# One product (h w_in) in four column groups, spread by DMAs, in place of four products and sixteen transposing ones

## The chip, the core and the metric

The kernel runs on one core of a Trainium2 chip. The metric is the device time of one execution in microseconds (us), the median of several runs. The engines are TensorE (PE, matmuls; PEld is its weight load), VectorE (DVE), ScalarE (ACT), GpSimd (POOL) and SyncE (SP), which here issues the DMAs.

## The reference

Three stages follow each other over N = 12480 tokens of width 128:

```
h   = mab(I, x)                 # 32 inducing points attend to all tokens
x1  = mab(x, h)                 # each token attends to the 32 rows of h
        mab(q, kv): s = (q kv^T) / sqrt(128); a = softmax(s) (sum + 1e-9); a kv
y1  = prelu(x1 w_in, alpha) w_out          # w_in 128 x 2048, w_out 2048 x 128
out = relu(y1 w2_in)^2 w2_out              # the same shapes
```

All is fp32. The weights arrive as float64 and are converted on the chip.

## The kernel before

**First attention.** Seven groups of tokens are loaded, transposed on PE into xT and attended to. Beside them the pieces of w_in and w_out are converted from float64 to float32: `convs[k]` holds for each piece the parts MAG, LOW (both ACT), BITS, SIGN (DVE), ADD (POOL), and for w_out also REST (POOL, the product with 1 - alpha), HI (ACT, the fp32r high part) and LO (POOL, the low part). `convs[4]` to `convs[7]` are the four pieces of w_out. At its end hT stands in SBUF: h transposed, 128 x 32, four times beside each other.

**Second attention folded into the first MLP.** Softmax weights a of a token over 32 rows make x1 = a h, so x1 w_in = a (h w_in). The kernel therefore makes w1s, the high and low fp32r parts of h w_in stacked on the partitions (rows 0 to 63 high, twice; rows 64 to 127 low, twice), and a_s, the high and low parts of a, stacked likewise; one fp32r matmul of the two (line 618, `l1_a`) gives a chunk of 128 hidden units for a tile of tokens. w1s is made in four pieces of 512 columns: `make_w1s(k)` is an fp32 product on PE (line 531), `split_w1s(k, 0)` a cast on ACT, `split_w1s(k, 1)` a subtraction on DVE (line 536). Piece 0 is made ahead of the main loop, the others in it.

**The linear part of the PReLU.** alpha goes through v = (h w_in) diag(alpha) w_out, 32 x 128. It needs (h w_in) transposed: `step_wa` makes that in sixteen fp32 products (line 548), `scale_wa` copies it (ACT) and multiplies by alpha (POOL), `step_v` (line 592) makes v, `copy_v` and `split_v` give v_s, and `end_y1` adds a_s v_s.

**second_attention(tiles)** is a list of steps: scores (PE), transpose (DVE, line 465), maximum and subtraction (lines 470, 472), exp (ACT, 475), sums (lines 480 to 482, the product at 484), transpose back (488) and, for several tiles, `step_split`: casts and low parts, and four DMAs per tile to a_s. `first` is tile 0 alone, cut into three parts of 128 tokens; it has `step_spread` (PE, line 512) and `step_split_spread` (lines 519, 521) in place of DMAs. `second` is tiles 1 to 3. In `step_max` the subtraction is on DVE for `first` and in the main loop, and on POOL otherwise.

**The main loop** runs over steps s. The order in each engine's queue is the order of the program. Step s issues `l1_a(s)` (chunk s % 16 of tile s // 16), from step 24 on `l2_a(s - 24)` (the second MLP's first half), and the second halves `l1_b` (three fp32r matmuls, lines 628 to 630) five and later three steps behind, and `l2_b`. Each `l1_a` writes one of four PSUM banks in its first 24 steps (h1 and h2, two each); ACT's relu (line 622) and DVE's subtraction (line 624) empty it. A table `plan`, filled by `at(step, f)`, adds other work at the end of a step. `PIECES` says at which steps the pieces of w2_in and w2_out are converted (parts at s, s+1, s+2 and s+6). Their raw data lie in four buffers, so that the load of a piece waits for the ADD of the piece four before it. All these loads and the DMAs to a_s go through SP's one queue, in order.

Of the kernel before, what the change touches and what calls it, by code (L numbers as in the profile page):

```python
# [19 lines left out]
T = 512  # L20
# [5 lines left out]
Q = 4  # L26
# [4 lines left out]
def attention_then_two_mlps(ctx: ExitStack, tc, x, inducing, w_in, w_out, alpha, w2_in, w2_out, out):  # L31
# [327 lines left out]
    for g in range(last):  # L359
# [48 lines left out]
    sums(last)  # L408
    nnm = att.tile([P, 73], F32, name="nnm", tag="nnm")[:, :1]
    nc.vector.tensor_scalar_mul(nnm, nm[last], -1.0)  # L410
# [24 lines left out]
        den.unsqueeze(1).to_broadcast([P, Q, M]), op=ALU.mult,  # L435
    )
    convs[5][REST]()
    convs[4][LO]()
    convs[7][BITS]()

# [3 lines left out]
    def second_attention(tiles, cuts=None):  # L444
# [32 lines left out]
        def step_sum():  # L477
            a = v["a"]
            sm = att.tile([P, 3 * T // M], F32, name="sm", tag="sm")[:n, : w // M]
            nc.vector.reduce_sum(sm, a, axis=AX.X)  # L480
            nc.vector.tensor_scalar_add(sm, sm, 1e-9)
            nc.vector.reciprocal(sm, sm)
            mult = nc.vector.tensor_tensor if cuts else nc.gpsimd.tensor_tensor
            mult(a, a, sm.unsqueeze(2).to_broadcast([n, w // M, M]), op=ALU.mult)
# [5 lines left out]
        def new_a_s(t):  # L490
            a_s[t] = columns(att.tile([P, T], F32R, name="a_s", tag="a_s", bufs=5), wide[t])
            return a_s[t]

        def step_split():

            hi = att.tile([P, T], F32R, name="a_hi", tag="a_hi")
            nc.scalar.copy(hi[:n, :w], v["t"][:n, :w])
            lo = att.tile([P, T], F32R, name="a_lo", tag="a_lo")
            pool_lo(lo[:n, :w], v["t"][:n, :w], hi[:n, :w])
            for i, t in enumerate(tiles):  # L500
                d = new_a_s(t)
                for k in range(4):
                    nc.sync.dma_start(
                        out=f32(d[k * M : (k + 1) * M]),
                        in_=f32((lo if k % 2 else hi)[i * M : (i + 1) * M, :w]),
                    )
# [9 lines left out]
        def step_split_spread():  # L516

            d = a_s[tiles[0]] = new_a_s(tiles[0])[: 3 * M]
            nc.scalar.copy(d, v["b"][: 3 * M, :tw])
# [6 lines left out]

    w1_bank = {}

    def make_w1s(k):
        w1_bank[k] = x_banks[k]() if k < 2 else y2_bank()  # L530
        nc.tensor.matmul(w1_bank[k], hT, w_in_sb[:, k * 512 : (k + 1) * 512], start=True, stop=True)

    def split_w1s(k, low):
        dst, b = w1s[:, k * 512 : (k + 1) * 512], w1_bank[k]
        if low:
            nc.vector.tensor_tensor(dst[64:], b[64:], f32(dst[64:]), op=ALU.subtract)  # L536
        else:
            nc.scalar.copy(dst, b)

    wa = att.tile([P, NCH, M], F32, name="wa", tag="a_s", bufs=5)  # L540
    wa_bank = []

    def step_wa(chunks):
        if not wa_bank:
            wa_bank.append(y2_bank())
        for c in chunks:
            n = min(P, (c + 1) * M)
            nc.tensor.matmul(
                wa_bank[0][:, (c + 1) * M - n : (c + 1) * M], w_in_sb[:, c * P : (c + 1) * P], hT[:, :n],
                start=True, stop=True,  # L550
            )

    def scale_wa():
        nc.scalar.copy(wa, wa_bank[0].rearrange("p (c j) -> p c j", j=M))
        nc.gpsimd.tensor_tensor(wa, wa, al.unsqueeze(2).to_broadcast([P, NCH, M]), op=ALU.mult)

    first = second_attention([0], [0, P, 2 * P])
    second = second_attention([1, 2, 3])
    first[0]()
    make_w1s(0)  # L560
    step_wa(range(15, 3, -1))
    run(first[1:4])
    split_w1s(0, 0)
    convs[5][HI]()
    stage1.close()
    run(first[4:6])
    split_w1s(0, 1)
    convs[6][SIGN]()
    first[6]()
    second[0]()  # L570
    first[7]()
    convs[7][SIGN]()
    convs[6][ADD]()
    convs[5][LO]()
    convs[6][REST]()
    second[1]()
    second[2]()
    convs[7][ADD]()
    convs[7][REST]()
    load_w("w2_in", 0)  # L580
    load_w("w2_in", 1)
    load_w("w2_out", 0)
    load_w("w2_in", 2)

# [3 lines left out]
    def step_v():  # L588
        v_bank.append(y2_bank())
        for c in range(NCH):  # L590
            q = c % Q
            nc.tensor.matmul(
                v_bank[0][q * M : (q + 1) * M, :P], wa[:, c, :], w_out_sb[:, c, :],
                start=(c < Q), stop=(c >= NCH - Q), tile_position=(0, q * M),
            )
# [80 lines left out]
    def l2_b(i):  # L676
# [21 lines left out]
    PIECES = [  # L698
        (8, "w2_in", 0), (13, "w2_in", 1), (18, "w2_out", 0), (21, "w2_in", 2),
        (23, "w2_out", 1), (25, "w2_in", 3), (28, "w2_out", 2), (32, "w2_out", 3),  # L700
    ]
# [5 lines left out]

    at(0, step_wa, range(3, -1, -1))
    at(0, make_w1s, 1)
    at(1, split_w1s, 1, 0)  # L710
    at(1, split_w1s, 1, 1)
    at(1, second[3])
    at(2, scale_wa)
    at(2, make_w1s, 2)
    at(2, split_w1s, 2, 0)
    at(2, convs[6][HI])
    at(2, convs[6][LO])
    at(3, second[4])
    at(4, split_w1s, 2, 1)
    at(5, second[5])  # L720
    at(5, make_w1s, 3)
    at(5, split_w1s, 3, 0)
    at(6, convs[7][HI])
    at(6, convs[7][LO])
    at(7, split_w1s, 3, 1)
    at(7, second[6])
    at(10, step_v)
# [83 lines left out]
```

## Time and profile before

| | us |
|---|---|
| median of 3 runs (lowest to highest) | 968.28 (968.27 to 969.36) |
| the profiled execution | 969.27 |
| its span in the trace | 967.5 |
| PE busy in the span | 954.3 |
| DVE busy | 658.3 |
| ACT busy | 728.5 |
| POOL busy | 535.4 |

The span is the time from the first to the last instruction of the trace; the profiled execution's own time is a little longer. Busy times are sums over the span. Matmuls overlap, and their ends in the trace are modelled, so PE's busy time is no measure of its peak. Every fp32 matmul appears as two instructions.

### The profile page before, as it was taken

The page shows a single profiled execution, that of the slowest core. Times are in us where ns is not written, and L with a number is a line of the kernel's source. Part 1 is how long each engine was busy: PE and PEld are TensorE (multiplying, and loading weights), DVE is VectorE, ACT ScalarE, POOL GpSimd, SP SyncE. Part 2 cuts the span into 40 slices and gives each one's busy share as a digit, 9 for nine tenths or more (in the row PEclk, how much of TensorE's full clock was granted, in tenths as well). Part 3 has the DMA queues.
Part 4 walks back from the last instruction along what each step waited for, and adds up shares of the span by engine and source line. Part 5 has one row for each costly group of instructions (what it writes and reads, how often), then busy time and mean ns, then how long its engine had stood idle before and what let it go on. Part 6 is the DMA issues. An engine that isn't in the chain of part 4 may idle for free.

```text
span 967.5 us, 13705 instructions
## 1 busy us (share of the span) xinstructions
PE 954.3 (99%) x4577; PEld 791.6 (82%) x4577; DVE 658.3 (68%) x1027; ACT 728.5 (75%) x1335; POOL 535.4 (55%) x438
## 2 busy tenths in 40 slices
PE   9989999999999999999999999999999999999997
PEld 7767899887888887888887888887888887888886
DVE  6878876666766666676666776666766666766677
ACT  6678787777777777777777777777777777777775
POOL 2458765555565555565555565555566555566520
PEclk9999999999999999999999999999999999999999
DMA  8531002000001000002000002000002000001001
GB/s 327 163 111 45 9 7 48 11 3 8 12 14 41 12 1 12 12 9 47 11 1 12 12 3 53 12 1 12 12 1 55 11 1 12 12 1 23 11 2 23
DMA packets 65159, 28.28 MB, mean 29 GB/s; under 512 B 53584, under 2 KB 58304, under 8 KB 65088
## 3 DMA queue, kind: packets, MB, share of 16 engines
q1 hardware_dynamic: 64032, 27.27, 11.3%
q8 instruction: 36, 0.59, 0.3%
q14 instruction: 35, 0.29, 0.1%
q10 hardware_dynamic: 1056, 0.13, 0.1%
HBM read 14.80 MB, written 6.39 MB: 22 GB/s over the span
## 4 chain that ended last, share of the span: by engine, by line
PE 96%; ACT 1%; DVE 1%; POOL 1%; issue 0%; DVEq 0%; ACTq 0%
PE y L630 18%; PE y L629 18%; PE y L628 18%; PE h L628 9%; PE h L630 9%; PE h L629 9%; PE h L618 9%; PE h L273 1%; PE ms L287 1%; PE ms L457 1%; PE y L646 1%; PE y L337 1%; ACT g1h L622 0%; DVE g1l L624 0%; PE ms L95 0%
## 5 line engine op out<-in xcount | busy, mean ns | idle before, releaser
L673 POOL TENSOR_TENSOR g2l<-sq,g2h 128x512 fp32r<-128x512 f32 (+2 forms) x376 | 474.0, 1261 | 345.9 <-ACT g2h L671 327.4
L624 DVE SCALAR_TENSOR_TENSOR g1l<-h,g1h 128x512 fp32r<-128x512 f32 (+2 forms) x400 | 269.6, 676 | 238.2 <-ACT g1h L622 232.3
L622 ACT ACTIVATE g1h<-h 128x512 fp32r<-128x512 f32 (+2 forms) x400 | 234.6, 588 | 151.1 <-PE h L618 149.0
L664 DVE TENSOR_TENSOR sq<-h,r 128x512 f32<-128x512 f32 (+2 forms) x400 | 270.8, 677 | 46.1 <-ACT r L662 7.5
L662 ACT ACTIVATE r<-h 128x512 f32<-128x512 f32 (+2 forms) x400 | 234.8, 587 | 59.0 <-PE h L630 12.5
L671 ACT CAST g2h<-sq 128x512 fp32r<-128x512 f32 (+2 forms) x400 | 240.2, 600 | 3.7 <-DVE sq L664 3.7
L618 PE MATMUL h<-a_s,w1s 128*128 128x512 f32 (+2 forms) x400 | 156.2, 391 | 4.4 <-DVE w1s L536 2.0
L628 PE MATMUL h<-y1h,w2i_hi 128*128 128x512 f32 (+2 forms) x400 | 154.3, 386 | 1.5 <-DVE g1l L624 1.5
L630 PE MATMUL y<-g1l,wo_hi 128*128 128x512 f32 (+2 forms) x400 | 154.2, 385 | 0.0
L629 PE MATMUL y<-g2h,w2o_lo 128*128 128x512 f32 (+2 forms) x400 | 153.7, 384 | 0.2 <-POOL w2o_lo L215 0.2
L628 PE MATMUL y<-g1h,wo_hi 128*128 128x512 f32 (+2 forms) x400 | 153.8, 385 | 0.0
L629 PE MATMUL y<-g1h,wo_lo 128*128 128x512 f32 (+2 forms) x400 | 153.8, 385 | 0.0
L630 PE MATMUL h<-y1l,w2i_hi 128*128 128x512 f32 (+2 forms) x400 | 153.7, 384 | 0.0
L628 PE MATMUL y<-g2h,w2o_hi 128*128 128x512 f32 (+2 forms) x400 | 153.6, 384 | 0.0
L629 PE MATMUL h<-y1h,w2i_lo 128*128 128x512 f32 (+2 forms) x400 | 153.6, 384 | 0.0
L630 PE MATMUL y<-g2l,w2o_hi 128*128 128x512 f32 (+2 forms) x400 | 153.6, 384 | 0.0
L618 PEld LDWEIGHTS h<-a_s,w1s 128*128 128x128 f32 (+1 forms) x400 | 75.1, 188 | 27.0 <-DVE sq L664 5.0
L628 PEld LDWEIGHTS h<-y1h,w2i_hi 128*128 128x128 f32 x400 | 75.1, 188 | 16.8 <-DVE g1l L624 1.9
L629 PEld LDWEIGHTS y<-g2h,w2o_lo 128*128 128x128 f32 x400 | 75.1, 188 | 15.3 <-POOL w2o_lo L215 0.5
L628 PEld LDWEIGHTS y<-g2h,w2o_hi 128*128 128x128 f32 x400 | 75.2, 188 | 14.7
L629 PEld LDWEIGHTS h<-y1h,w2i_lo 128*128 128x128 f32 x400 | 75.1, 188 | 14.6
L630 PEld LDWEIGHTS y<-g2l,w2o_hi 128*128 128x128 f32 x400 | 75.1, 188 | 14.0 <-DVE g2l L673 0.2
(134 smaller groups left out, 688.5 us busy)
## 6 DMA issues: line engine op xcount, KB each, us to landing
out_dram<-o SPq DMA_DIRECT2D x82, 64.0 KB, 2.0
raw<-in_moe_w_in_dram SPq DMA_DIRECT2D x8, 512.0 KB, 5.2
xg<-in_x_dram SPq DMA_DIRECT2D x8, 512.0 KB, 9.2
raw<-in_moe_w_out_dram SPq DMA_DIRECT2D x8, 512.0 KB, 4.1
a_s<-a_hi SPq DMA_DIRECT2D x42, 64.0 KB, 2.0
a_s<-a_lo SPq DMA_DIRECT2D x42, 64.0 KB, 2.0
xg<-in_x_dram SPq DMA_DIRECT2D x4, 256.0 KB, 3.7
x_last<-in_x_dram SPq DMA_DIRECT2D x2, 512.0 KB, 10.6
```

What stands on the lines that cost most here:

```text
L273: nc.tensor.transpose(b[:, k * p : (k + 1) * p], x_t[g][:p, i, k, :], ident[:p, :p])
L287: nc.tensor.matmul(b[i * M : (i + 1) * M, :n], indT, xT[:, t0 : t0 + n], start=True, stop=True, tile_position=(0, i * M),)
L618: nc.tensor.matmul(b[:, :w], w1s[: a.shape[0], c * P : (c + 1) * P], a, start=True, stop=True)
L622: nc.scalar.activation(hi, b[:, :w], AF.Relu)
L624: nc.vector.scalar_tensor_tensor(lo, b[:, :w], 0.0, f32(hi), op0=ALU.max, op1=ALU.subtract)
L628: nc.tensor.matmul(b, w_hi, hi, start=start, stop=False)
L629: nc.tensor.matmul(b, w_lo, hi, start=False, stop=False)
L630: nc.tensor.matmul(b, w_hi, lo, start=False, stop=stop)
L662: nc.scalar.activation(r, b, AF.Relu)
L664: nc.vector.tensor_tensor(sq, b, r, op=ALU.mult)
L671: nc.scalar.copy(hi, sq)
L673: (nc.vector if i >= total - LAG2 else nc.gpsimd).tensor_tensor(lo, sq, f32(hi), op=ALU.subtract)
```

## The change

The product (h w_in) is made once more compactly. Piece 0 of w1s is made as before. All four pieces are also made by four fp32 matmuls with 32 columns of hT, each in a column group of PE of its own, so that piece k stands on partitions 32k to 32k + 31 of one bank. ACT copies this bank to `w1f` (fp32) and `w1h` (fp32r), POOL makes the low part `w1l`. Nine DMAs on SP's queue bring pieces 1 to 3 to w1s (high, high, low for each). The transposed form for alpha comes from four PE transposes of `w1f`, and `scale_wa` is one DVE product that reads PSUM. w1s and a_s have 96 rows in place of 128 (high, high, low against high, low, high), so `step_split` sends three DMAs per tile. Around it, SIGN, ADD, REST and HI of piece 6 and BITS of piece 7 move to other places, transpose, maximum and subtraction of tiles 1 to 3 move into steps 0 and 1 of the loop, five idle products (`keep_busy(5)`) are added, and the w2 pieces start up to two steps earlier.

```diff
     convs[5][SIGN]()
...
+    convs[6][SIGN]()
     convs[5][REST]()
     convs[4][LO]()
-    convs[7][BITS]()
+    convs[6][ADD]()
+    convs[6][REST]()
...
-                for k in range(4):
+                for k in range(3):
                     nc.sync.dma_start(
                         out=f32(d[k * M : (k + 1) * M]),
...
+    def make_first_w1s():
+        w1["first"] = h1_bank()
+        nc.tensor.matmul(w1["first"], hT, w_in_sb[:, :512], start=True, stop=True)
+
+    def make_w1():
+        b = w1["bank"] = h2_bank()
+        for k in range(Q):
+            nc.tensor.matmul(
+                b[k * M : (k + 1) * M], hT[:, :M], w_in_sb[:, k * 512 : (k + 1) * 512], start=True, stop=True,
+                tile_position=(0, k * M),
+            )
+
+    def first_w1s_low():
+        nc.vector.tensor_tensor(w1s[64:, :512], w1["first"][64:], f32(w1s[64:, :512]), op=ALU.subtract)
+
+    def copy_w1():
+        nc.scalar.copy(w1s[:, :512], w1["first"])
+        w1["f"] = att.tile([P, 512], F32, name="w1f", tag="a_s", bufs=5)
+        nc.scalar.copy(w1["f"], w1["bank"])
+        w1["hi"] = att.tile([P, 512], F32R, name="w1h", tag="a_s", bufs=5)
+        nc.scalar.copy(w1["hi"], w1["bank"])
+        w1["lo"] = att.tile([P, 512], F32R, name="w1l", tag="a_s", bufs=5)
+        pool_lo(w1["lo"], w1["f"], w1["hi"])
+
+    def spread_w1s():
+        for k in range(1, Q):
+            for r, v in enumerate(("hi", "hi", "lo")):
+                nc.sync.dma_start(
+                    out=f32(w1s[r * M : (r + 1) * M, k * 512 : (k + 1) * 512]), in_=f32(w1[v][k * M : (k + 1) * M, :])
+                )
+
+    def step_wa():
+        b = w1["wa"] = y2_bank()
+        for q in range(Q):
+            nc.tensor.transpose(b[:, q * P : (q + 1) * P], w1["f"][:, q * P : (q + 1) * P], ident)
+
     def scale_wa():
-        nc.scalar.copy(wa, wa_bank[0].rearrange("p (c j) -> p c j", j=M))
-        nc.gpsimd.tensor_tensor(wa, wa, al.unsqueeze(2).to_broadcast([P, NCH, M]), op=ALU.mult)
+        wa = w1["wa scaled"] = att.tile([P, Q, Q, M], F32, name="wa", tag="a_s", bufs=5)
+        nc.vector.tensor_tensor(
+            wa, w1["wa"].rearrange("p (q k j) -> p q k j", q=Q, k=Q),
+            al.rearrange("p (k q) -> p q k", q=Q).unsqueeze(3).to_broadcast([P, Q, Q, M]), op=ALU.mult,
+        )
...
     first[0]()
-    make_w1s(0)
-    step_wa(range(15, 3, -1))
+    make_first_w1s()
+    make_w1()
     run(first[1:4])
-    split_w1s(0, 0)
+    copy_w1()
+    keep_busy(5, idle_bank)
     convs[5][HI]()
+    run(first[4:6])
+    step_wa()
     stage1.close()
-    run(first[4:6])
-    split_w1s(0, 1)
-    convs[6][SIGN]()
+    first_w1s_low()
+    convs[7][BITS]()
     first[6]()
     second[0]()
     first[7]()
     convs[7][SIGN]()
-    convs[6][ADD]()
-    convs[5][LO]()
-    convs[6][REST]()
-    second[1]()
-    second[2]()
-    convs[7][ADD]()
-    convs[7][REST]()
+    convs[6][HI]()
     load_w("w2_in", 0)
     load_w("w2_in", 1)
     load_w("w2_out", 0)
+    spread_w1s()
+    convs[5][LO]()
+    convs[7][ADD]()
+    convs[7][REST]()
+    convs[6][LO]()
     load_w("w2_in", 2)
...
     PIECES = [
-        (8, "w2_in", 0), (13, "w2_in", 1), (18, "w2_out", 0), (21, "w2_in", 2),
-        (23, "w2_out", 1), (25, "w2_in", 3), (28, "w2_out", 2), (32, "w2_out", 3),
+        (7, "w2_in", 0), (11, "w2_in", 1), (16, "w2_out", 0), (20, "w2_in", 2),
+        (22, "w2_out", 1), (25, "w2_in", 3), (28, "w2_out", 2), (32, "w2_out", 3),
     ]
...
-    at(0, step_wa, range(3, -1, -1))
-    at(0, make_w1s, 1)
-    at(1, split_w1s, 1, 0)
-    at(1, split_w1s, 1, 1)
-    at(1, second[3])
+    at(0, second[1])
+    at(1, second[2])
+    at(2, second[3])
     at(2, scale_wa)
-    at(2, make_w1s, 2)
-    at(2, split_w1s, 2, 0)
-    at(2, convs[6][HI])
-    at(2, convs[6][LO])
     at(3, second[4])
-    at(4, split_w1s, 2, 1)
+    at(4, convs[7][HI])
+    at(4, convs[7][LO])
     at(5, second[5])
-    at(5, make_w1s, 3)
-    at(5, split_w1s, 3, 0)
-    at(6, convs[7][HI])
-    at(6, convs[7][LO])
-    at(7, split_w1s, 3, 1)
-    at(7, second[6])
+    at(6, second[6])
     at(10, step_v)
```

## Rows read from the trace of the kernel before

**Rows 1.** Busy time of each engine by stretch: us, (instructions), clock, DMA.
```profile
52.00:56.00 4.00, 2.11 (x10) 1.38 (x9) 3.35 (x7) 3.01 (x8) 3.62 (x5) 1.00 0.39 125
56.00:60.00 4.00, 4.00 (x36) 3.32 (x39) 3.72 (x8) 2.84 (x6) 1.99 (x2) 0.65 0.10 23
...
200.00:400.00 200.00, 200.00 (x891) 164.11 (x890) 131.98 (x194) 150.58 (x269) 113.69 (x89) 1.00 0.07 12
```

**Rows 2.** PE in order of time: start, us, engine, line, operation [idle before, releaser].
```profile
39.72 1.13 PE L531 MATMUL h<-w_in_sb,hT 128*128 128x512 f32 x2
...
40.69 2.84 PE L548 MATMUL y<-hT,w_in_sb 128*128 128x128 f32 x24
...
44.20 0.95 PE L457 MATMUL ms<-xT,hT 128*32 128x448 f32 x6
...
45.42 0.44 PE L618 MATMUL h<-a_s,w1s 96*128 96x384 f32 x1 [0.27 <-DVE a_s L521]
...
55.84 0.41 PE L618 MATMUL h<-a_s,w1s 96*128 96x384 f32 x1 [1.73 <-DVE w1s L536]
...
58.91 1.87 PE L592 MATMUL y<-w_out_sb,wa 128*32 128x128 f32 x32
...
64.55 0.36 PE L618 MATMUL h<-a_s,w1s 128*128 128x448 f32 x1
...
73.31 0.44 PE L628 MATMUL h<-y1h,w2i_hi 128*128 128x384 f32 x1 [1.50 <-DVE g1l L624]
```

**Rows 3.** DVE in order of time, 39 to 56 us.
```profile
39.24 0.98 DVE L203 TENSOR_SCALAR mag<-mag 128x512 int32<-128x512 int32 x1
...
40.79 0.69 DVE L472 TENSOR_TENSOR a<-a,mx 96x128 f32<-96x128 f32 x1
...
42.18 0.17 DVE L481 TENSOR_SCALAR sm<-sm 96x4 f32<-96x4 f32 x1
...
42.59 0.29 DVE L484 TENSOR_TENSOR a<-a,sm 96x128 f32<-96x128 f32 x1
...
43.97 0.69 DVE L207 SCALAR_TENSOR_TENSOR mag<-raw,mag 128x512 int32<-128x512 int32 x1
...
45.39 1.24 DVE L207 SCALAR_TENSOR_TENSOR mag<-raw,mag 128x512 int32<-128x512 int32 x1
...
46.66 0.65 DVE L465 STREAM_TRANSPOSE a<-ms 96x448 f32<-96x448 f32 x1
...
47.34 0.61 DVE L470 TENSOR_REDUCE mx<-a 96x14 f32<-96x448 f32 x1
...
47.88 1.03 DVE L624 SCALAR_TENSOR_TENSOR g1l<-h,g1h 128x384 fp32r<-128x384 f32 x2
...
53.65 0.66 DVE L481 TENSOR_SCALAR sm<-sm 96x14 f32<-96x14 f32 x1
...
55.00 0.69 DVE L536 TENSOR_TENSOR w1s<-y,w1s 64x512 fp32r<-64x512 f32 x1
```

**Rows 4.** ACT in order of time, the cast of the first piece of w1s.
```profile
41.74 0.56 ACT L538 CAST w1s<-h 128x512 fp32r<-128x512 f32 x1
```

**Rows 5.** POOL in order of time, 38 to 55 us.
```profile
38.89 1.04 POOL L225 TENSOR_TENSOR aw<-w_out_sb,al 128x512 f32<-128x512 f32 x1
...
39.89 1.45 POOL L215 TENSOR_TENSOR wo_lo<-aw,wo_hi 128x512 fp32r<-128x512 f32 x1
...
44.80 1.28 POOL L210 TENSOR_TENSOR w_out_sb<-mag,raw 128x512 int32<-128x512 int32 x1 [3.46 <-ACT a_s L519]
...
53.00 1.28 POOL L215 TENSOR_TENSOR wo_lo<-aw,wo_hi 128x512 fp32r<-128x512 f32 x1
```

**Rows 6.** SP queue in order of time: one DMA of 56 KB to a_s.
```profile
59.24 0.58 SPq L503 DMA_DIRECT2D a_s<-a_hi  x1
```

**Rows 7.** DMA issues: operation, count, KB each, median us to landing.
```profile
a_s<-a_hi SPq DMA_DIRECT2D x42, 64.0 KB, 2.0
...
al_raw<-in_moe_alpha_dram SPq DMA_DIRECT2D x1, 8.0 KB, 8.2
```

More of the change, by code (lines that the diff above doesn't have):

```diff
@@ L408, in attention_then_two_mlps @@
     sums(last)
-    nnm = att.tile([P, 73], F32, name="nnm", tag="nnm")[:, :1]
+    nnm = att.tile([P, 57], F32, name="nnm", tag="nnm")[:, :1]
     nc.vector.tensor_scalar_mul(nnm, nm[last], -1.0)
@@ L478, in step_sum @@
             a = v["a"]
-            sm = att.tile([P, 3 * T // M], F32, name="sm", tag="sm")[:n, : w // M]
+            sm = att.tile([P, 4 * T // M], F32, name="sm", tag="sm")[:n, : w // M]
             nc.vector.reduce_sum(sm, a, axis=AX.X)
@@ L490, in new_a_s @@
         def new_a_s(t):
-            a_s[t] = columns(att.tile([P, T], F32R, name="a_s", tag="a_s", bufs=5), wide[t])
+            a_s[t] = columns(att.tile([P, T], F32R, name="a_s", tag="a_s", bufs=5), wide[t])[: 3 * M]
             return a_s[t]
@@ L516, in step_split_spread @@
         def step_split_spread():
-            d = a_s[tiles[0]] = new_a_s(tiles[0])[: 3 * M]
+            d = new_a_s(tiles[0])
             nc.scalar.copy(d, v["b"][: 3 * M, :tw])
@@ L524, in second_attention @@
         return steps + ([step_spread, step_split_spread] if cuts else [step_split])
[L527 to L547, printed above, removed]
+    w1 = {}
+    def make_first_w1s():
[4 more added lines that the diff above has]
+        for k in range(Q):
             nc.tensor.matmul(
-                wa_bank[0][:, (c + 1) * M - n : (c + 1) * M], w_in_sb[:, c * P : (c + 1) * P], hT[:, :n],
-                start=True, stop=True,
-            )
@@ L592, in step_v @@
             nc.tensor.matmul(
-                v_bank[0][q * M : (q + 1) * M, :P], wa[:, c, :], w_out_sb[:, c, :],
+                v_bank[0][q * M : (q + 1) * M, :P], w1["wa scaled"][:, q, c // Q], w_out_sb[:, c, :],
                 start=(c < Q), stop=(c >= NCH - Q), tile_position=(0, q * M),
```

## The prediction

> **What bounds the kernel now.** I read the page first, which puts TensorE (PE) on nearly all of the chain that ended last, then the busy time by stretch. The reader is to see there that from about 104 us on PE is busy all the time at full clock (200.00 of 200 us in the row shown), so nothing that the other engines do there can shorten the run, and that PE is short of work at the start of the main loop: in 52 to 56 us it worked 2.11 of 4, and in 56 to 60 the granted clock was 0.65, which costs 4 x 0.35 = 1.4 us of its full speed [rows 1]. So the change is worth what it does to the start of the main loop. Then the timelines. The loop's first matmul (line 618) stands at 45.42, released by VectorE (DVE), not by PE; the first chunk of token tile 1 (step 16) comes at 64.55, and the first of the second MLP (step 24) at 73.31 [rows 2]. Whatever moves these points and is not given back before 104 us moves the end by as much.
>
> Steps 0 to 16 take 64.55 - 45.42 = 19.13 us. PE's own step is four matmuls: between the end of step_v (58.91 + 1.87 = 60.78) and 64.55 lie five steps and split_v, 0.75 us each [rows 2]. Sixteen would be 12.0 us. The rest is fp32 work of the old w1s and wa products, one wait of 1.73 us for the low half of a w1s piece, and waits for banks, which DVE empties at 1.03 / 2 = 0.5 us per chunk [rows 2, 3].
>
> **What goes.** On PE, inside the loop: three 512-column products (line 531, 1.1 us each with their end) and four of line 548; 24 instructions of it, 12 products, took 2.84, so 0.24 each, 0.95 for four [rows 2]. Together 3 x 1.1 + 0.95 = 4.2 us. On DVE, three lows of 0.69 = 2.1 us [rows 3]. On ScalarE (ACT), three casts of 0.56 and the copy of wa, 2.2 us [rows 4]. On POOL the product of wa with alpha. The wait of 1.73 goes with its cause.
>
> **What comes.** PE ahead of the loop: one 512-column product (1.1), four column groups (the scores of line 457, three groups of 448 columns in six instructions, took 0.95 in all [rows 2]; I take 1.1 for four of 512; one after another would be 4.4, and the six-instruction row excludes it), five idle products at 0.24 and four transposes (between nothing and 0.95, the price of the four products of line 548; I take 0.5). They end near 43.6 and have to be done before the spread of tile 0, which I put at 44.7 below: hidden. Before, twelve products and one of line 531 filled the same gap, so PE was not the limit there either. ACT makes three copies in place of one, 0.56 each, from 42.1 to 43.6, in a stretch in which it waits for the next a_s: hidden. In the loop DVE gets scale_wa (PSUM and SBUF input, bounded by 0.49 and 0.69 of rows of that kind; I take 0.69) and the subtraction of the tiles 1 to 3 (no longer on POOL; 96 x 448, own time near the 0.65 of the transpose of that shape), and the transpose and maximum of these tiles (0.65, 0.61) move into the loop's queue from a place just ahead of it [rows 3]. DVE's balance in the loop is 0.69 + 0.65 - 2.1 = -0.8 us.
>
> **The prologue's chain gets longer.** This is the step that I weigh most. DVE instructions that read only SBUF are long exactly when POOL is at work. The shift of line 203 at 39.24 took 0.98 and ended 0.29 after POOL's product of 38.89 (at 39.93); the subtraction at 40.79 took 0.69 for 96 x 128 and ended at 41.48, just after POOL's low half ended at 41.34, while the product of the same shape at 42.59, with POOL idle, took 0.29; the sign step takes 0.69 at 43.97, POOL idle, and 1.24 at 45.39, POOL busy; the small tensor_scalar of line 481 takes 0.17 at 42.18 and 0.66 at 53.65, ending at 54.31 where POOL ended at 54.28 [rows 3, 5]. In the kernel before, POOL is idle from 41.34 to 44.80 (3.46 us), which is where the chain of tile 0 runs [rows 5]. The change fills this gap: ADD and REST of piece 6 and the low half of w1 go to POOL there, and the 0.69 sign step stands on DVE in front of the chain. Walking it: the sign step gets through at 39.8 and ends at 40.5 (the shift ended at 40.22); POOL's low half ends at 41.6 in place of 41.34, the subtraction at 41.8, exp at 42.1; line 481 waits for ADD's end at 43.0 (before: 42.35), line 484 waits for REST's end at 44.05 and ends at 44.2 (before: 42.88). The loop's first matmul stood 2.54 after that end (45.42 - 42.88); I take off 0.1, since the products of line 548, which end at 43.53, no longer stand in front of the spread: 44.2 + 2.44 = 46.6. If nothing of this bites it comes at 45.2, the sign step being shorter than the held shift. These are the ends, +1.2 and -0.2; I take +1.2, because every such row beside a busy POOL is long.
>
> The Trainium skill, "SBUF — State Buffer", section "Who interferes with whom", says that a VectorE instruction with two SBUF inputs or in a two-port mode and a GpSimd instruction lock each other out for a whole instruction, and that one with a PSUM input does not contend. The rows above agree (0.29 against 0.69, 0.17 against 0.66); by the rule the chain is 1.2 us later, without it 0.2 earlier, and scale_wa, which reads PSUM, would be free of it.
>
> **The nine DMAs.** The queue of SP issues one such transfer per 0.6 us and it lands 2.0 us later [rows 6, 7]. Ahead of them stands the load of w2_out 0, which waits for ADD of piece 6 at 43.0, no longer for 46.1. The low half of w1 is done on POOL at 45.5; its first transfer goes then, with the two high ones out before. Group 1 lands at 47.5, group 2 at 49.3, group 3 at 51.1. Steps 4, 8 and 12 need them. The nearest worse row is the 8 KB transfer that took 8.2 us behind large loads [rows 7]: then group 1 lands near 53.8.
>
> **The loop.** DVE in order from 46.5: the sign step of piece 7, held by POOL to 47.1, ends at 47.7; bank 0 at 48.2; transpose 48.85; bank 1 at 49.35; maximum 49.9; subtraction, held to 50.05, 50.65; bank 2 at 51.15; scale_wa 51.85; bank 3 at 52.35; sums 53.35; bank 4 at 53.85. Banks are reused after four chunks, so PE does step 4 at 48.3 (group 1 is there, 0.8 us ahead) and step 8 at 53.9; before, step 8 stood at 55.84, after the wait. From there PE is the limit: eight steps of 0.75 and step_v, 1.87 at the lower clock of its row and half of it, 0.9, at the full one, which end at 60.8 to 61.8; I take 61.4. PE works less than half of 47 to 54 us, less than in 52 to 56 of before, which came just ahead of the lower clock; so I expect a stretch at 1.2 GHz here too and charge 0.8 for it, near the middle of nothing and 1.4 [rows 1]. Step 16 at 62.2: 2.3 us earlier than 64.55.
>
> **After step 16.** The conversions of w2 start one or two steps earlier. Their work is the same and PE's 8.76 us to step 24 contain waits of 1.50 and others; I credit 0.5, between nothing (conversions still crowd DVE) and 1.5 (the wait at 73.31 goes [rows 2]). Three rows of a_s per tile in place of four saves SP's time alone: PE is full there, and a matmul over 96 rows costs what one over 128 costs (0.44 at 45.42, 0.36 for a wider one at 64.55 [rows 2]). Later groups: nothing.
>
> **Sum.** -2.3 - 0.5 = -2.8 us. The profiled execution took 969.27, its span and 1.77 around it; so 966.5 there. The median of the runs is 0.99 below the profiled one: 968.28 - 2.8 = 965.5.
>
> **Rivals.** (1) POOL does not hold the chain: 1.4 us more gained, 964.1, and 963.3 if the clock stays up as well. For it: the five long rows overlap POOL only by my reading of their ends. Against: every overlapped SBUF-only row is long. 0.2. (2) The gain is given back to the clock: the first stretch costs its whole 1.4 (0.6 more than charged) and a second one as much; 965.5 + 2.0 = 967.5. For it: PE idles more in 47 to 54 us than before. Against: from step 8 on it has work without end. 0.2. (3) Slower: the spread lands late. Group 1 decides: it has 0.8 us to spare, and from there each microsecond delays step 4 and the fourteen behind it. At 53.8, twelve steps at 0.75 and step_v at 0.9 end at 63.7, with two low stretches at 66.5, up to 2 us later than before: 970. Against: the a_s transfers, of the same size, take 2.0 us in the median [rows 7]. 0.1. My forecast holds 0.5, with a range of its own of 964.2 to 966.8.
>
> **Chances.** 0.2% is 1.94 us, about what can be told from no change here; the border stands at 966.3. Rival 1 and most of the forecast (0.42) are faster: 0.62. Rival 2 and the rest of the forecast: 0.28 same. Rival 3: 0.10 slower. The range leaves out rival 3 and the lower part of rival 1: 963.0 to 968.5.
>
> **What would show it.** In the profile after: line 484 of tile 0 ends near 44.2 and not at 42.9; first line 618 near 46.6; no fp32 product of the w1s or wa kind after it; step 16 near 62; step 24 near 70.5; from 104 us nothing changed. The prediction is wrong if step 4 waits for w1s from a DMA, if the clock is low for over 4 us, or if the conversions make new waits between steps 16 and 40.

## The result and the profile after

The change made the kernel slower: 976.89 us in the median against 968.77, ratio 1.0083 (95% interval 1.0066 to 1.0101). The forecast was 965.5. The profiled execution took 976.8 us, its span is 975.0, 7.5 longer than before.

Busy time by stretch, of the changed kernel (columns as in [rows 1]):

```profile
52.00:56.00 4.00, 2.93 (x9) 2.83 (x10) 3.93 (x9) 2.60 (x6) 0.80 (x2) 0.50 0.46 131
56.00:60.00 4.00, 4.00 (x44) 3.76 (x43) 2.42 (x5) 3.09 (x7) 2.60 (x3) 0.70 0.08 20
...
200.00:400.00 200.00, 200.00 (x882) 162.73 (x881) 131.01 (x192) 149.26 (x266) 112.41 (x89) 1.00 0.06 11
```

The last row matters most. PE is busy all the time, at full clock, and waits for nobody, as before [rows 1]; but in the same 200 us it did 882 matmuls and not 891. The busy share cannot show that; the count can.

PE in order of time, of the changed kernel (line 636 is the loop's first matmul, 618 before; 646 to 648 are 628 to 630; 610 is step_v):

```profile
47.69 0.96 PE L636 MATMUL h<-a_s,w1s 96*128 96x384 f32 x4 [1.00 <-DVE a_s L523]
49.30 0.44 PE L636 MATMUL h<-a_s,w1s 96*128 96x384 f32 x1 [0.66 <-DVE g1l L642]
...
55.80 0.52 PE L636 MATMUL h<-a_s,w1s 96*128 96x384 f32 x1
...
59.19 1.08 PE L610 MATMUL y<-w_out_sb,wa 128*32 128x128 f32 x32
...
64.04 0.37 PE L636 MATMUL h<-a_s,w1s 96*128 96x448 f32 x1
...
72.76 0.45 PE L646 MATMUL h<-y1h,w2i_hi 128*128 128x384 f32 x1 [0.22 <-DVE g1l L642]
...
300.94 0.39 PE L648 MATMUL y<-g2l,w2o_hi 128*128 128x512 f32 x1
301.16 0.40 PE L636 MATMUL h<-a_s,w1s 96*128 96x512 f32 x1
301.40 0.40 PE L646 MATMUL h<-y1h,w2i_hi 128*128 128x512 f32 x1
301.63 0.40 PE L647 MATMUL h<-y1h,w2i_lo 128*128 128x512 f32 x1
301.87 0.39 PE L648 MATMUL h<-y1l,w2i_hi 128*128 128x512 f32 x1
302.10 0.39 PE L646 MATMUL y<-g1h,wo_hi 128*128 128x512 f32 x1
```

Step 16 comes at 64.04 and step 24's second MLP at 72.76, 0.5 us earlier than before each [rows 2]. The last six rows show where the time went: the matmul of 96 rows and the three behind it start 0.23 to 0.24 apart. Over 17 steps from 300 us on, the mean from one start to the next is 0.232, 0.237, 0.233 and 0.230 us behind these four, and 0.227 behind the other six; in the kernel before it is 0.227 behind all ten.

Starts of the loop's first matmul, read off the timelines of the two kernels:

| step | before, us | after, us | difference |
|---|---|---|---|
| 0 | 45.42 | 47.69 | +2.27 |
| 8 | 55.84 | 55.80 | -0.04 |
| 16 | 64.55 | 64.04 | -0.51 |
| 48 | 122.48 | 121.43 | -1.05 |
| 96 | 224.60 | 223.74 | -0.86 |
| 112 | 262.34 | 261.92 | -0.42 |
| 392 | 906.21 | 913.59 | +7.38 |

The product on DVE that writes hT (line 433) comes ahead of every instruction that the change moves or adds, and does not stand at the same place in the two executions either. First the kernel before, then the changed one:

```profile
39.03 0.29 DVE L433 TENSOR_TENSOR hT<-y,den 128x128 f32<-128x128 f32 x1
```

```profile
39.24 0.29 DVE L433 TENSOR_TENSOR hT<-y,den 128x128 f32<-128x128 f32 x1
```

So the start gained 1.05 us, 1.26 if counted from hT, and from about step 96 on, once both MLPs work on tiles of 512 columns, each step costs more: (913.59 - 261.92) / 280 = 2.3274 us from step 112 to 392, against 2.2995. That is 0.0279 more, 7.8 us in these 280 steps. In steps 48 to 64, with 448 columns, it was 0.008.

Between step 64 and 96 the difference hardly moves, though the changed kernel has its 96 rows there too. Tiles of 512 and of 448 columns alternate in these steps. PE in order of time, of the kernel before:

```profile
163.19 0.39 PE L618 MATMUL h<-a_s,w1s 128*128 128x512 f32 x1
163.42 0.37 PE L628 MATMUL h<-y1h,w2i_hi 128*128 128x448 f32 x1
...
164.04 0.39 PE L628 MATMUL y<-g1h,wo_hi 128*128 128x512 f32 x1
...
164.73 0.37 PE L628 MATMUL y<-g2h,w2o_hi 128*128 128x448 f32 x1
...
171.81 0.40 PE L618 MATMUL h<-a_s,w1s 128*128 128x512 f32 x1
```

From the first to the last of these rows are four steps of 2.155 us. Four matmuls of 512 columns at 0.2267 and six of 448 at 0.2000, their prices among their like, make 2.107. So the kernel before already loses 0.05 us per step here, with 128 rows everywhere, and the changed one takes 2.153 per step. That the alternating widths cause the loss is read from these rows; no run tried it.

### The profile page after: what moved, and what is told of

Read it like the earlier page. It is cut to its first block, busy times and chain, and to the rows that moved or that the text cites. A ratio compares the mean times of both kernels' runs of the same rounds, so it can differ in the third digit from the quotient of the medians.

```text
span 975.0 us, 13667 instructions
## 1 busy us (share of the span) xinstructions
PE 960.8 (99%) x4561; PEld 792.1 (81%) x4561; DVE 659.2 (68%) x1026; ACT 728.5 (75%) x1333; POOL 535.7 (55%) x437
## 3 DMA queue, kind: packets, MB, share of 16 engines
HBM read 14.80 MB, written 6.39 MB: 22 GB/s over the span
## 4 chain that ended last, share of the span: by engine, by line
PE 96%; DVE 2%; ACT 1%; issue 1%; POOL 0%; DVEq 0%; ACTq 0%
PE y L646 18%; PE y L647 18%; PE y L648 18%; PE h L646 9%; PE h L647 9%; PE h L636 9%; PE h L648 9%; PE h L273 1%; PE ms L287 1%; PE ms L459 1%; PE y L664 1%; PE y L337 1%; DVE g1l L642 0%; ACT g1h L640 0%; DVE mag L207 0%
## 5 line engine op out<-in xcount | busy, mean ns | idle before, releaser
L636 PE MATMUL h<-a_s,w1s 96*128 96x512 f32 (+2 forms) x400 | 157.9, 396 | 5.5 <-DVE g1l L642 4.5
L646 PE MATMUL h<-y1h,w2i_hi 128*128 128x512 f32 (+2 forms) x400 | 157.5, 394 | 1.0 <-DVE g1l L642 1.0
L636 PEld LDWEIGHTS h<-a_s,w1s 96*128 96x128 f32 x400 | 75.6, 189 | 26.9 <-DVE g1l L642 6.9
L648 PEld LDWEIGHTS h<-y1l,w2i_hi 128*128 128x128 f32 x400 | 75.1, 188 | 16.0
L646 PEld LDWEIGHTS y<-g1h,wo_hi 128*128 128x128 f32 x400 | 75.8, 190 | 14.8
L647 PEld LDWEIGHTS y<-g1h,wo_lo 128*128 128x128 f32 x400 | 75.7, 189 | 14.5
## 6 DMA issues: line engine op xcount, KB each, us to landing
x_last<-in_x_dram SPq DMA_DIRECT2D x2, 512.0 KB, 10.2
```

The costliest lines, as they stand in the source:

```text
L636: nc.tensor.matmul(b[:, :w], w1s[: a.shape[0], c * P : (c + 1) * P], a, start=True, stop=True)
L646: nc.tensor.matmul(b, w_hi, hi, start=start, stop=False)
L647: nc.tensor.matmul(b, w_lo, hi, start=False, stop=False)
L648: nc.tensor.matmul(b, w_hi, lo, start=False, stop=stop)
```

## The experiments

Kernels named b_ are the kernel before with an edit, those named a the changed one. All ratios are to the kernel before on the same chip; its own median was 968.6 to 969.4 in these comparisons. The kernels ran on different chips, so a difference between two of them is taken from the ratios as well as from the medians.

### The rows of the contraction

**b_l1_96**, one line of the kernel before:

```diff
-        nc.tensor.matmul(b[:, :w], w1s[: a.shape[0], c * P : (c + 1) * P], a, start=True, stop=True)
+        nc.tensor.matmul(b[:, :w], w1s[:96, c * P : (c + 1) * P], a[:96], start=True, stop=True)
```

> The kernel before, with one edit: the first matmul of each main-loop step (line 618) contracts 96 rows of w1s and a_s in place of 128; everything else, four DMAs per tile too, stays. It leaves out the product of the two low parts. Theory A (the 96-row matmul itself slows TensorE: in the trace after, a step of 512 columns takes 2.295 us against 2.267, 0.028 more in some 300 steps): about 8.5 us slower, near 977.3, and the step 2.29 to 2.30 us. Theory B (the loss after 104 us comes from something else in the change: addresses of tiles, fewer DMAs, other times of transfers): within 1 us of before, step 2.27.

977.41 us, ratio 1.0088 (1.0074 to 1.0101); 2.3261 per step from step 112 to 392. Busy time by stretch:

```profile
56.00:60.00 4.00, 4.00 (x48) 3.39 (x49) 3.69 (x8) 2.99 (x7) 2.08 (x2) 1.00 0.07 17
...
200.00:400.00 200.00, 200.00 (x882) 162.80 (x881) 131.06 (x192) 149.36 (x266) 112.47 (x89) 1.00 0.07 12
```

The same 882 matmuls as in the changed kernel, and the whole of its loss, from this one line. Theory A holds, B falls. The first row shows something else: this kernel starts with the same instructions as the one before, but in this execution the clock did not fall (1.00 in place of the 0.65 of [rows 1]), and step 16 came at 63.18, 1.4 us earlier.

**a_128**, the opposite edit:

```diff
-            a_s[t] = columns(att.tile([P, T], F32R, name="a_s", tag="a_s", bufs=5), wide[t])[: 3 * M]
+            a_s[t] = columns(att.tile([P, T], F32R, name="a_s", tag="a_s", bufs=5), wide[t])
...
-                for k in range(3):
+                for k in range(4):
...
-            for r, v in enumerate(("hi", "hi", "lo")):
+            for r, v in enumerate(("hi", "hi", "lo", "lo")):
```

> The changed kernel with 128 rows again: four DMAs per tile to a_s and twelve, not nine, to w1s, so that the main loop's first matmul contracts 128 rows except in tile 0. Theory A: the step of 512 columns goes back to 2.267, and what is left is the start, which was 1.05 us ahead at step 48: 967.5 to 968.5, a little faster than before. Theory B: still near 976.

967.51 us, ratio 0.9983 (0.9975 to 0.9992), 2.2995 per step, 1.09 ahead of before from step 48 to the end. The rest of the change is a small gain.

**b_all_96** puts 96 rows into lines 618 and 628 to 630.

> The kernel before with 96 rows in line 618 and in the three matmuls of lines 628 to 630, that is in all ten matmuls of a step; it leaves out the last quarter of the contraction in each. A1 (a matmul that follows or precedes one of another number of rows pays, 28 ns per step for the one odd matmul): no change of rows is left, so within 1 us of before. A2 (every 96-row matmul costs more by itself, 7 to 28 ns): ten of them cost 70 to 280 ns per step, 25 to 100 us slower.

971.47 us, ratio 1.0027 (1.0017 to 1.0038), 2.3013 per step. Busy time by stretch:

```profile
104.00:108.00 4.00, 4.00 (x17) 3.81 (x16) 1.73 (x4) 2.37 (x5) 2.50 (x4) 0.67 0.00 0
...
200.00:400.00 200.00, 200.00 (x891) 164.10 (x890) 132.07 (x194) 150.45 (x268) 113.34 (x89) 1.00 0.07 12
```

Back to 891 matmuls: a matmul of 96 rows among its like costs what one of 128 costs. A2 falls. The profiled execution lost 2.35 us against before between steps 36 and 48, where the clock stood at 0.67, after a stretch of 0.91; A1's "within 1 us" missed that. The executions of this kernel spread from 968.92 to 974.82 us. The one of 968.92 is the only one of ten whose mean clock was 1.00, and the executions of before with 1.00 on this chip took 968.0 to 968.4. Why the clock falls at these places is not shown.

**b_l1_l2_96** puts them into line 618 and the three matmuls of l2_a behind it.

> The kernel before with 96 rows in the first matmul of a step (line 618) and in the three of l2_a that follow it; it leaves out the last quarter of the contraction of the second MLP's first half. Four matmuls of 96 rows, but as many changes between 96 and 128 rows as with one. A1 (the change of rows costs): as with line 618 alone, 2.293 per step, near 977.4. A2 (each 96-row matmul beside 128-row ones costs): up to four times 0.027 per step, 985 to 1003. A3 (what follows a 96-row matmul with 128 rows is what gets slow, three of them): the same as A1 or a little less, with the longer intervals now behind the l2_a matmuls.

982.08 us, ratio 1.0134 (1.0120 to 1.0148), 2.3394 per step: 0.040 more than before, where one odd matmul costs 0.027. Neither the same, as A1 in its simple form said, nor four times as much. From one start to the next it is 0.232, 0.235, 0.228 and 0.232 behind the four, and then 0.234, 0.233 and 0.231 behind the next three, those of 128 rows. So each change of rows, from 128 to 96 and from 96 to 128, slows the next three or four matmuls, by some 0.02 us in sum; where the two stand side by side, as in the changed kernel, the sum is 0.027 and not twice as much.

**b_l1_64** takes 64 rows in line 618.

> The kernel before with 64 rows in line 618 in place of 128; it leaves out the low part of w1s. If any number of rows that differs from its neighbours' costs the same: near 977 as with 96 rows. If it grows with the rows that are missing: near 985. If only 96, which is no power of two, is slow: near 968.8.

1117.64 us, ratio 1.1535 (1.1519 to 1.1550): none of the three. PE in order of time, and under it the weight loads of the same stretch:

```profile
321.34 0.39 PE L630 MATMUL y<-g2l,w2o_hi 128*128 128x512 f32 x1
321.66 0.50 PE L618 MATMUL h<-a_s,w1s 64*128 64x512 f32 x1
322.08 0.50 PE L628 MATMUL h<-y1h,w2i_hi 128*128 128x512 f32 x1
322.42 0.39 PE L629 MATMUL h<-y1h,w2i_lo 128*128 128x512 f32 x1
```

```profile
321.12 0.19 PEld L630 LDWEIGHTS y<-g2l,w2o_hi 128*128 128x128 f32 x1
321.65 0.18 PEld L618 LDWEIGHTS h<-a_s,w1s 64*128 64x128 f32 x1 [0.35 <-issue]
322.08 0.19 PEld L628 LDWEIGHTS h<-y1h,w2i_hi 128*128 128x128 f32 x1 [0.24 <-DVE sq L664]
```

Here the weight load no longer runs under the matmul in front: it starts at 321.65, and its matmul at 321.66. The same again on the way back. Two gaps, 0.40 per step in all (2.667 against 2.267 in the steps from 300 us on). With 96 rows (b_l1_96) each load still starts with the matmul in front of its own, 0.22 to 0.24 ahead, and only 0.027 us per step are lost.

### The start of the loop

The eleven programs, that of before and the changed one included, are the same on DVE up to the product that writes hT. In these executions it stands between 38.73 and 39.99, 39.71 in a_128. A difference between two kernels at one step holds that of hT, so the steps are also counted from hT; a table at the end of this section has them all.

**a128_pool_gap** is a_128 with SIGN, ADD, REST of piece 6 and BITS of piece 7 back in their old places:

```diff
-    convs[6][SIGN]()
     convs[5][REST]()
     convs[4][LO]()
-    convs[6][ADD]()
-    convs[6][REST]()
+    convs[7][BITS]()
...
     first_w1s_low()
-    convs[7][BITS]()
+    convs[6][SIGN]()
...
     convs[7][SIGN]()
+    convs[6][ADD]()
+    convs[6][REST]()
```

> The changed kernel with 128 rows, and SIGN, ADD and REST of piece 6 and BITS of piece 7 back where they stood before, so that POOL is free again while the chain of tile 0 runs on VectorE. Theory A (POOL's work holds the chain): line 486 of tile 0 takes 0.3 us, not 0.99, and the loop's first matmul comes at 45.4 to 45.8 us in place of 48.15. Theory A1: this is worth its 2.4 us, 965.1. Theory A2 (the loop's start is then set by the work that now stands in the queues of POOL and VectorE, and by the w1s transfers behind ADD): step 16 stays near 64, 967 to 968. Rival B (the chain is not held by POOL): first matmul still near 48.

967.90 us, ratio 0.9991 (0.9983 to 1.0000). DVE in order of time, then SP's queue, then PE:

```profile
43.10 0.29 DVE L484 TENSOR_TENSOR a<-a,sm 96x128 f32<-96x128 f32 x1
```

```profile
47.07 0.38 SPq L178 DMA_DIRECT2D raw<-in_moe_w_out_dram  x1
47.54 1.22 SPq L556 DMA_DIRECT2D w1s<-w1h  x2
```

```profile
46.31 0.96 PE L636 MATMUL h<-a_s,w1s 96*128 96x384 f32 x4 [0.65 <-DVE a_s L521]
52.62 0.98 PE L636 MATMUL h<-a_s,w1s 96*128 96x384 f32 x2 [5.35 <-DVE a L472]
```

With POOL idle the product takes 0.29, not 0.99, and the loop starts 1.84 us earlier than in a_128, 1.65 counted from hT. That is less than the 2.4 expected: the sign step in front of the low part of a_s now meets POOL's low part of w1 and takes 1.19. Then PE waits 5.35 us: the load in front of the transfers on SP's queue had to wait for ADD of piece 6, now late, and so the transfers left at 47.54, where those of the changed kernel left at 43.80. The profile names line 472 of DVE as the releaser, which happened to end at 52.55. What step 4 needs of DVE, the first emptied bank, was there at 50.12; the first of the transfers took 4.5 us to land, until 52.0, and the others of its group followed. That is A2, and the late spread of the prediction's third rival, by way of a queue.

**a128_gap_first** puts `spread_w1s()` ahead of `load_w("w2_out", 0)`, and BITS of piece 7 behind the low part of a_s.

> As a128_pool_gap, with the twelve transfers to w1s ahead of the load of w2_out 0 in SP's queue, and BITS of piece 7 behind the low part of a_s. There step 4 stood at 52.62 after 5.35 us of waiting, because the load waited for ADD of piece 6 (done at 47.0) and the transfers stood behind it. Theory A (order in SP's queue is what ate the gain): the transfers start at 44 to 45, step 0 comes near 45.7, step 4 near 48.5, step 16 near 61.5; 965.5 to 966.5, 1.5 to 2.4 better than with the load ahead. Rival (the queue of POOL is what is late, since ADD and REST of pieces 6 and 7 now follow each other from 45.7 on): step 4 early, but step 16 still near 64, 967 to 968.

967.86 us, ratio 0.9982 (0.9974 to 0.9991); step 4 at 50.19, step 16 at 64.81. The transfers left at 44.08 and step 4 came 2.9 us earlier than in a128_pool_gap, counted from hT, but step 48 did not (82.12 behind hT against 81.95): the rival's outcome. In this execution the clock stood at 0.50 for 10.2 us, from 49.3 on, in a_128 and a128_pool_gap for 6.8. ACT in order of time:

```profile
48.53 0.62 ACT L230 CAST wo_hi<-aw 128x512 fp32r<-128x512 f32 x1 [2.79 <-POOL aw L225]
49.06 1.24 ACT L640 ACTIVATE g1h<-h 128x384 fp32r<-128x384 f32 x3
```

The cast of HI waits for REST on POOL, and the first relu stands behind it. **a128_gap_hi_later** moves HI and LO of piece 6 to step 2.

> As a128_gap_first, with HI and LO of piece 6 at the end of step 2, where they stood before the change. In a128_gap_first the cast of HI on ScalarE stood ahead of the loop's first relu and waited 2.79 us for REST on POOL, so that the banks of steps 0 to 3 were emptied from 49.57 on and step 4 stood at 50.19. Theory A (each earlier arrival of tile 0 was eaten by the next instruction queued behind POOL's later work): now step 4 comes near 48.2 to 48.8, step 16 at 62 to 63 and the run is 1.5 to 2.5 us faster than a128_gap_first, 965.5 to 966.5. Rival (VectorE's sign steps of pieces 6 and 7, held by POOL to 49.05, are late enough themselves): step 4 at 49.7 or later, 967 to 968.

967.01 us, ratio 0.9982 (0.9973 to 0.9991); step 4 at 49.03, step 16 at 63.67. DVE in order of time:

```profile
45.91 1.04 DVE L203 TENSOR_SCALAR mag<-mag 128x512 int32<-128x512 int32 x1
46.98 1.41 DVE L207 SCALAR_TENSOR_TENSOR mag<-raw,mag 128x512 int32<-128x512 int32 x1
48.42 0.56 DVE L640 SCALAR_TENSOR_TENSOR g1l<-h,g1h 128x384 fp32r<-128x384 f32 x1
```

Between the two theories in the trace, 0.5 earlier than a128_gap_first at step 48, counted from hT and with the clock low for the same 10.2 us; the ratio is the same. ACT no longer blocks, but BITS and SIGN take 2.45 us beside a busy POOL and the first bank is emptied from 48.42 on. POOL's work did not go away, so the instructions that it holds are now these. **a128_gap_busy** is a128_gap_first with the idle products told below.

> a128_gap_first with the idle products of steps 0 to 7. Theory A: 0.9 us better than without them, about 964.5 to 965.5, the clock at 1.00 throughout. Rival: the products delay the steps 0 to 8 by as much as the clock gives back, no difference within 0.5.

967.39 us, ratio 0.9978 (0.9968 to 0.9988), the clock at 1.00: 0.5 better than a128_gap_first on the same chip, where the executions of either spread by more than 1 us. That is the rival's "within 0.5"; in the trace it is 0.8 at step 48, counted from hT.

**a128_bits_later** is a_128 with one instruction moved:

```diff
     first_w1s_low()
-    convs[7][BITS]()
     first[6]()
     second[0]()
     first[7]()
+    convs[7][BITS]()
     convs[7][SIGN]()
```

> The changed kernel with 128 rows, and BITS of piece 7 behind the low part of a_s on VectorE. It took 1.55 us there, held by two POOL instructions, and the low part of a_s waited for it. Theory A: the first matmul comes 0.7 to 0.8 us earlier, at 47.4, and step 4 too; whether the end gains 0.7 depends on what VectorE does next, since BITS still has to be done: 966.8 to 967.5. Rival: no change of step 0, because the cast of a_s on ScalarE is what comes last.

966.12 us, ratio 0.9973 (0.9963 to 0.9983): better than expected. DVE in order of time:

```profile
43.20 1.00 DVE L486 TENSOR_TENSOR a<-a,sm 96x128 f32<-96x128 f32 x1
...
46.14 0.55 DVE L523 TENSOR_TENSOR a_s<-y,a_s 32x384 fp32r<-32x384 f32 x1 [0.87 <-ACT a_s L521]
46.72 0.43 DVE L203 TENSOR_SCALAR mag<-mag 128x512 int32<-128x512 int32 x1
47.18 0.69 DVE L207 SCALAR_TENSOR_TENSOR mag<-raw,mag 128x512 int32<-128x512 int32 x1
...
50.01 0.81 DVE L474 TENSOR_TENSOR a<-a,mx 96x448 f32<-96x448 f32 x1
```

BITS takes 0.43 here, in a pause of POOL, and no longer delays a_s; the subtraction of the tiles 1 to 3, which meets POOL at another time, takes 0.81, not 1.75. Step 16 comes at 61.96 and step 48 at 119.31, 2.1 ahead of a_128. hT stands 0.7 earlier here, so the move is worth 1.4 us at step 48; the medians differ by as much (967.51 and 966.12), the ratios by 1.0 us.

**a128_sub_on_pool** leaves this subtraction on POOL (`if cuts or tiles[0] > 1`).

> The changed kernel with 128 rows, and the subtraction of the maximum of tiles 1 to 3 on POOL as before. On VectorE it took 1.75 us at step 1, held by POOL, and the banks of steps 2 and 3 waited behind it. Theory A: step 6 comes 1.7 us earlier than 53.53 and step 8 at 54.6, step 16 about 1 us earlier: 966.5. Rival: POOL is the limit there (its own low part ends at 52.5), exp of these tiles comes later than now and the a_s transfers with it, so nothing is gained or step 16 waits for a_s: 967.5 to 968.5.

968.61 us, ratio 0.9999 (0.9990 to 1.0008): the rival. POOL comes to it at 52.66, ACT's exp stands at 53.62 with the relus of steps 3 on behind it, and step 16 falls back to 66.65. (The profiled execution took 970.41, the longest of ten.)

**a128_busy** is a_128 with idle products in steps 0 to 7:

```diff
+    def busy():
+        if "idle" not in w1:
+            w1["idle"] = y2_bank()
+        for _ in range(3):
+            nc.tensor.matmul(w1["idle"][:, :P], same, same, start=True, stop=True)
+
+    for k in range(8):
+        at(k, busy)
```

> The changed kernel with 128 rows, and three idle fp32 products of 128 columns (0.24 us each) at the end of each of the steps 0 to 7, in a bank of their own. Theory A (the granted clock of 0.50 from 51 to 57.7 us follows on TensorE's idle time from 47 to 53 us, and it holds steps 6 to 10 back): the clock stays at 1.00, step 16 comes 1 to 2 us earlier, 965.5 to 966.5. Rival (VectorE's emptying of banks sets the pace there anyway, and the products stand in the way): 967.5 to 969, even with the clock up.

967.00 us, ratio 0.9985 (0.9976 to 0.9993). The clock stayed up:

```profile
52.00:56.00 4.00, 4.00 (x31) 4.00 (x30) 3.69 (x9) 2.38 (x7) 2.42 (x3) 1.00 0.65 170
```

Step 16 came at 63.17, 1.0 earlier, step 48 at 120.52, 0.9 earlier, but about half of that is hT's: counted from hT it is 0.5 and 0.4. That is less than theory A's 1 to 2, and the ratios of the two kernels do not tell them apart. It is what the clock gives less what the products take; step 4 comes 1.8 later with them. With BITS later as well, **a128_bits_busy**:

> The changed kernel with 128 rows, BITS of piece 7 later (2.1 us ahead of a_128 at step 48) and the idle products of steps 0 to 7 (0.9 ahead). Theory A (two separate losses, a wait on VectorE and the lower clock): they add up, step 48 at 118.4 to 118.8, 965.0 to 965.5. Rival (bits later gained through the phase of the lower clock, and the products take its place): no better than bits later alone, 966 or more.

966.11 us, ratio 0.9967 (0.9955 to 0.9980), step 48 at 119.23 against 119.31, and 0.2 later counted from hT: the rival. The products hold step 4 up by 1.6 us, and at full clock that is nearly made up by step 16. What the clock alone is worth there, this run cannot tell.

Counted from hT, in us:

| kernel | hT | step 0 | step 4 | step 16 | step 48 |
|---|---|---|---|---|---|
| before | 39.03 | 6.39 | 10.66 | 25.52 | 83.45 |
| the changed kernel | 39.24 | 8.44 | 10.06 | 24.80 | 82.19 |
| a_128 | 39.71 | 8.44 | 10.06 | 24.45 | 81.68 |
| a128_pool_gap | 39.52 | 6.79 | 13.10 | 24.65 | 81.95 |
| a128_gap_first | 39.99 | 6.59 | 10.19 | 24.82 | 82.12 |
| a128_gap_hi_later | 39.33 | 6.60 | 9.70 | 24.34 | 81.63 |
| a128_gap_busy | 39.63 | 6.60 | 10.20 | 24.17 | 81.34 |
| a128_bits_later | 39.03 | 7.71 | 9.49 | 22.93 | 80.29 |
| a128_sub_on_pool | 39.86 | 8.46 | 10.07 | 26.79 | 84.06 |
| a128_busy | 39.24 | 8.44 | 11.84 | 23.93 | 81.27 |
| a128_bits_busy | 38.73 | 7.70 | 11.10 | 23.19 | 80.50 |

## Why the prediction was wrong

**The step that failed** is the sentence "a matmul over 96 rows costs what one over 128 costs", and with it "Later groups: nothing". Among its like it does (b_all_96). Between matmuls of 128 rows it costs 0.027 to 0.028 us per step of 512 columns, and that comes in some 300 of the 400 steps: 8.4 us from step 96 to the last, more than all the start could give. It is most of the 11.4 us between 965.5 and 976.89; the start fell short of its 2.8 by 1.5 (1.26 counted from hT), and the rest is mostly the reference, below. One line reproduces it (b_l1_96), and the opposite edit takes it away (a_128). The rows of before that I compared, 0.44 at 45.42 and 0.36 at 64.55 [rows 2], are durations with modelled ends, one of them in a stalled stretch; what counts is the distance between starts of back-to-back matmuls. None of my rivals was of that kind, because I looked for what the change does to waits, and PE waits for nothing there. What in PE's pipeline makes a change of rows cost is not shown by these runs.

**The chain held by POOL** was right: line 486 of tile 0 ended at 44.40 where I had put 44.2, with hT 0.21 later in this execution. What I mis-sized stands behind it. DVE in order of time, of the changed kernel, and then POOL:

```profile
43.41 0.99 DVE L486 TENSOR_TENSOR a<-a,sm 96x128 f32<-96x128 f32 x1
...
44.78 0.69 DVE L544 TENSOR_TENSOR w1s<-h,w1s 64x512 fp32r<-64x512 f32 x1
45.50 1.55 DVE L203 TENSOR_SCALAR mag<-mag 128x512 int32<-128x512 int32 x1
47.08 0.55 DVE L523 TENSOR_TENSOR a_s<-y,a_s 32x384 fp32r<-32x384 f32 x1
...
50.80 1.75 DVE L474 TENSOR_TENSOR a<-a,mx 96x448 f32<-96x448 f32 x1
```

```profile
43.22 1.04 POOL L225 TENSOR_TENSOR aw<-w_out_sb,al 128x512 f32<-128x512 f32 x1
44.22 1.31 POOL L215 TENSOR_TENSOR w1l<-w1f,w1h 128x512 fp32r<-128x512 f32 x1
45.49 1.28 POOL L215 TENSOR_TENSOR wo_lo<-aw,wo_hi 128x512 fp32r<-128x512 f32 x1
...
50.80 1.27 POOL L215 TENSOR_TENSOR wo_lo<-aw,wo_hi 128x512 fp32r<-128x512 f32 x1
```

The 2.44 from there to step 0 I took over from before, where POOL was mostly idle; they have no term for BITS of piece 7, which now stands in front of the low part of a_s. BITS began at 45.50, as w1l ended and POOL's next instruction began (45.49), and took 1.55 where it takes 0.43 in a pause of POOL (a128_bits_later); the low part of a_s came at 47.08 and step 0 at 47.69, 0.9 later than the 46.6 of the sum if hT's 0.21 is taken off. Without BITS there, and with hT at 39.03 as in before, step 0 stood at 46.74. The subtraction, counted as held for 0.15, met POOL in the same instant and was held for about 1.1. The Trainium skill, "SBUF — State Buffer", section "Who interferes with whom", says of an instruction in a two-port mode that whoever issues first gets the shared ports for the whole instruction and the other is blocked. The two pairs of rows agree in that each instruction takes 1.0 to 1.1 longer beside one of POOL of 1.3 (the subtraction takes 0.71 in a128_gap_hi_later); which began first, rows 0.01 apart cannot show. a128_bits_later, where both meetings are gone or shorter, shows what they were worth: 1.4 us at step 48.

**The loop.** The new products cost what was charged: the four column groups took 1.07 us in all, the transposes 0.66. The transfers were in time, as forecast (step 4 was released by a bank). The clock fell as forecast, for about seven microseconds (51.6 to 58.4) and not the four that I had named as the limit; a128_busy, without the fall, is 0.4 ahead at step 48 with its products in the way, where I had charged 0.8. Step 8 stood at 55.80 and not at 53.9, mostly from the two held instructions (54.07 in a128_bits_later). The sum of the start, -2.8, came out as -1.05 in the changed kernel, -1.09 in a_128 and -3.17 in a128_bits_later at step 48; counted from hT, as -1.26, -1.77 and -3.16. My reference was also soft: the one profile of before has a fall of the clock that another execution of the same start has not, worth 1.2 us at step 48 (121.31 in b_l1_96 against 122.48). The sum took its gain from that profile and set it against the median of 968.28, which by its times belongs to executions without the fall: in the comparison with b_l1_96, those of before with a mean clock of 1.00 took 968.0 to 968.4, those with 0.997 took 968.3 to 970.1. So about 1.2 us of the gain were counted twice.

**The conversions.** Credited with 0.5; between step 16 and 48 the changed kernel gained 0.54 (from -0.51 to -1.05), a_128 0.70. The size is luck. The upper end of the credit was the wait of 1.50 at step 24, but up to step 36 the changed kernel had lost 0.41 of its lead; it gained 1.04 between steps 36 and 40, where before waits twice (0.15 and 0.47 us) and the changed kernel does not. That the earlier conversions did it was not tried by itself.

**The rivals.** The first falls with the product of line 486, 0.99 beside POOL and 0.29 without (a128_pool_gap). The second's 967.5 is also a_128's median, by chance: there was no second low stretch, and the gain went to the held instructions. The third, slower through the late spread, gave the right sign by the wrong mechanism: in the changed kernel no step waited for a transfer. In a128_pool_gap it did.

## What to carry to other kernels

Where PE is busy without a pause, compare the distances between starts of back-to-back matmuls, or the count per stretch, and not busy time or durations; and give all matmuls of a dense loop the same number of rows, padding if need be. Before POOL work is moved into a gap, ask which VectorE instructions with SBUF operands alone will meet it, and put those behind the chain; one such move gave 1.0 to 1.4 us here (a_128 to a128_bits_later), and a kernel faster than both, at 0.9973 of before. When a chain is freed by moving work out of it, follow that work into every queue: it held up SP, then ACT, then DVE.

## What the runs showed of the hardware

- Among matmuls of 512 columns, a change between 128 and 96 rows from one to the next costs some 0.02 us each way, spread over the next three or four, and 0.027 for both where a single matmul differs; ten matmuls of 96 rows in a row cost no more than ten of 128. With 448 columns a single one costs 0.008, and where tiles of 512 and 448 columns alternate it costs nothing more (2.153 against 2.155 us per step).
- A change between 128 and 64 rows costs 0.40 us there and back; in these rows the weight load starts with its own matmul and no longer with the one in front.
- A VectorE instruction that reads only SBUF and begins with a POOL instruction of 1.3 us takes 1.0 to 1.1 longer (1.55 against 0.43, 1.75 against 0.71). One that reads PSUM is not held: the low part of the first w1s piece takes 0.69 at 44.78 beside a busy POOL in the changed kernel, and 0.69 at 43.25 with POOL idle in the kernel before.
